# A new order of events and new buffer places for a fused delta-rule attention and FFN kernel, with 30 instead of 49 groups of products of zeros

## The chip, the cores and the metric

The kernel runs on one core of one Trainium2 chip. The metric is the device time of one execution in microseconds (us). Before the change three runs took 625.97, 626.17 and 628.18 us; the median is 626.17 us.

## The reference

The inputs are q, k, v of shape (4, 8, 768, 48), beta (4, 8, 768), and two weights, w_in (384, 2048) and w_out (2048, 384). They come as float64 words that the kernel takes apart itself.

```python
k_n = k / (norm(k, axis=-1) + 1e-6)
for t in range(S):                       # S = 768
    y[:, :, t] = q[:, :, t] @ state      # 48 x 48 state for each of 32 heads
    v_old = state^T k_n[:, :, t]
    state = state + beta_t * outer(k_n[:, :, t], v_t - v_old)
x = y, heads side by side, (3072, 384)
h = x @ w_in
sp = where(h > 20, h, log1p(exp(min(h, 20))))
out = (h * tanh(sp)) @ w_out
```

So: a delta-rule recurrence over 768 tokens, and a feed-forward layer (FFN) with a mish activation behind it.

## The kernel before

**Tiling.** The recurrence is cut into 12 chunks of 64 tokens, n = 0 to 11. The 32 heads lie in two halves of 16 (h = 0, 1 stand for eight head pairs each). For a chunk the steps are: `s_a` and `s_b` (products ta and tb, the two parts of a triangular inverse), `s_gq` (products gq of k with the state and q), `s_z` (products pz of the inverse with v), `s_y` (products py, the attention output), `s_s` (products ps, the state's update) and `s_pg` (products pg of k with k). The state of chunk n lies in the tiles xx0 and xx1, one for each half; the gq of chunk n+1 reads what ps of chunk n has put there.

**Solves.** `early(g)` (L1403) solves the triangular systems of the two chunks 2g and 2g+1 together on VectorE: it turns the k of both chunks (L1411), adds up their pg products into d (L1397), transposes d into gt (L1447), and runs a chain of multiplications and additions (pr at L1494, gt at L1496), closes with a multiplication (L1498) and transposes back (L1516 and following); copies on GpSimd (`place`, L1535) bring the result to where pz reads it. "Solve 1" is early(1), for chunks 2 and 3.

**FFN.** `moe(n)` (L1822) does a chunk's 256 rows in eight parts fp: `g1` makes the products h (18 of them, 128x256, L1842), ScalarE makes e = mish(h) (L1857) and a rounded copy g (L1858), VectorE the remainder (L1859); `g2` adds 12 products acc (128x384, L1876). h0_1 is part 1 of chunk 0, and g2.0_1 or "the first acc" is named in the same way. The attention output is split for it into x0 (L1756, ScalarE) and x1 (L1757, VectorE).

**Weights.** `convert` (L1285) makes two float32 parts of each float64 weight tile: ri is a piece of w_in, ro of w_out. A clip (L1292), for some a rounding (L1300), a shift (L1305) and a combination (L1309) run on VectorE, the rest on ScalarE, GpSimd and, through products with an identity, on TensorE (L1321, L1325). These conversions stand between the first chunk's attention steps.

**Evictions.** gq is taken out by VectorE (L1712, L1715), pz by ScalarE in two copies (L1737), ps by VectorE (L1783; for chunk 0 by ScalarE), q of chunk 1 is turned by VectorE (L1615).

**Order.** Each engine runs its instructions in the order in which the program issues them. That order is a table: `TT` (L37) gives each event (a load, a conversion, a step with its attention and FFN parts, an eviction) its places in the whole program, and `SLOT` gives each tile its buffer in its pool. `put` pushes the pieces of an event with their place on a heap, and `run` (L2096) takes them off in that order; a piece whose `needs` are not given yet waits until they are. `load` (L1231) issues nearly all loads on SyncE's queue. `keep_warm` (L1900) issues products of a tile of zeros, whose result nobody reads, at the places that TT gives to the groups in `TN['warm']`:

```python
for _ in range(n):
    nc.tensor.matmul(warm, zb[:, 0:P], zb[:, :512], start=True, stop=True)
```

Of the kernel before, what the change touches and what calls it, by code (L numbers as in the profile page):

```python
# [29 lines left out]
def bcast_in(ap, n):  # L30
# [106 lines left out]
    'ats_gq[0,1].0>2': [160],
    'cv7': [161, 194, 201, 238, 239, 277, 335, 346, 968],
    'cv27': [162, 186, 243, 314, 560, 563, 572, 573, 577],
    'loadp': [169],  # L140
    'ats_a[0,1]': [170],
    'ats_a[0,0]': [171],
    'ats_a[0,1].0>1': [172],
    'warm11.9': [173],
# [2003 lines left out]
```

## Time and profile before

| | |
|---|---|
| median of three runs | 626.17 us |
| the profiled execution | 628.7 us |
| its span | 627.0 us |
| mean granted TensorE clock | 0.977 |
| TensorE (PE) busy | 588.8 us, 94% |
| VectorE (DVE) busy | 401.5 us, 64% |
| ScalarE (ACT) busy | 271.7 us, 43% |
| GpSimd (POOL) busy | 89.1 us, 14% |

The profile is one execution, taken by the hardware profiler; its span runs from the first to the last instruction, and 1.7 us of the execution's time lie around it. PE is TensorE, DVE VectorE, ACT ScalarE, POOL GpSimd, SP (and SPq, its queue) SyncE. PEclk is the clock that the throttle granted, as a part of full speed. A busy TensorE need not be at its peak. A time on an engine that others don't wait for costs nothing. Lines such as L1411 are lines of the kernel before; the changed kernel's lines behind its tables are lower by 19.

### The profile page before, as it was taken

How to read it: one execution, taken by the hardware profiler on the slowest of the kernel's cores; microseconds unless marked ns; L12 is line 12 of the kernel's file. 1: busy time of each engine (PE TensorE's matmuls, PEld its weight loads, DVE VectorE, ACT ScalarE, POOL GpSimd, SP SyncE). 2: the span in 40 equal slices, each digit the busy share in tenths (PEclk: the TensorE clock that was granted, in tenths of full speed). 3: DMA queues.
4: the chain of work that ended last, by engine and by line, in shares of the span. 5: the costliest groups of instructions: out<-in, count | busy, mean ns of one | idle time of the engine just before them, and what ended most of it. 6: DMA issues, size and time to landing. Idle time of an engine off the chain costs nothing.

```text
span 627.0 us, 22002 instructions
## 1 busy us (share of the span) xinstructions
PE 588.8 (94%) x9622; PEld 546.0 (87%) x9634; DVE 401.5 (64%) x873; ACT 271.7 (43%) x515; POOL 89.1 (14%) x142
## 2 busy tenths in 40 slices
PE   7679788998999999999999999999999999999997
PEld 5346577998899889998988998899999999999997
DVE  2898578997589966898465996456985434331110
ACT  4358748554443354424434434344333432333331
POOL 5120123315020030012101012101002110000000
PEclk9699979998999989999999999999999999999999
DMA  9998854862431421321523402420204121110011
GB/s 252 252 278 192 149 99 72 123 101 52 62 53 28 74 45 23 63 49 15 86 40 55 85 1 40 71 49 3 51 2 78 27 48 33 26 28 1 1 25 26
DMA packets 161775, 43.21 MB, mean 69 GB/s; under 512 B 149008, under 2 KB 157664, under 8 KB 161680
## 3 DMA queue, kind: packets, MB, share of 16 engines
q1 hardware_dynamic: 156640, 36.93, 30.5%
q0 software_dynamic: 2784, 4.29, 4.2%
q8 instruction: 76, 1.25, 0.8%
q10 hardware_dynamic: 2256, 0.59, 0.4%
q14 instruction: 19, 0.16, 0.1%
HBM read 32.87 MB, written 4.72 MB: 60 GB/s over the span
## 4 chain that ended last, share of the span: by engine, by line
PE 62%; DVE 18%; DMA 6%; ACT 4%; SPq 4%; issue 4%; POOL 1%; DVEq 0%; ACTq 0%; POOLq 0%
PE acc L1876 24%; PE h L1842 20%; DVE pr L1494 4%; DVE gt L1496 4%; SPq L1233 4%; PE py L1626 3%; PE pz L1626 3%; PE gq L1626 3%; DVE g L1859 2%; PE ps L1791 2%; PE pg L1393 1%; DMA kt<-in_k_dram 1%; DVE d L1516 1%; DMA ri<-in_moe_w_in_dram 1%; POOL tt L1535 1%
## 5 line engine op out<-in xcount | busy, mean ns | idle before, releaser
L1876 PE MATMUL acc<-wo,g 128*128 128x384 f32 x1152 | 217.9, 342 | 1.0 <-issue 1.0
L1842 PE MATMUL h<-x,wi 128*128 128x256 f32 x1728 | 217.2, 282 | 1.5 <-ACT e L1857 1.5
L1842 PEld LDWEIGHTS h<-x,wi 128*128 128x128 f32 x1728 | 209.8, 189 | 4.3 <-ACT e L1857 2.0
L1876 PEld LDWEIGHTS acc<-wo,g 128*128 128x128 f32 x1152 | 200.6, 190 | 4.8 <-issue 2.3
L1859 DVE TENSOR_TENSOR g<-e,g 128x512 fp32r<-128x512 f32 x96 | 66.4, 696 | 77.9 <-ACT g L1858 77.6
L1857 ACT ACTIVATE e<-h 128x512 f32<-128x512 f32 x96 | 57.0, 598 | 130.6 <-PE h L1842 97.6
L1858 ACT CAST g<-e 128x512 fp32r<-128x512 f32 x96 | 59.0, 620 | 28.4 <-PE acc L1876 25.9
L1494 DVE TENSOR_TENSOR pr<-gt 128x58 f32<-128x58 f32 (+9 forms) x164 | 56.6, 345 | 4.3
L1496 DVE TENSOR_TENSOR gt<-gt,pr 128x58 f32<-128x58 f32 (+9 forms) x164 | 54.7, 333 | 4.7
L1626 PE MATMUL gq<-xx,kt 48*64 48x112 f32 (+1 forms) x768 | 52.0, 273 | 2.8 <-issue 1.6
L1626 PEld LDWEIGHTS pz<-vt,tt 64*64 64x64 f32 x768 | 44.0, 135 | 7.7 <-issue 2.3
L1626 PE MATMUL pz<-vt,tt 64*64 64x48 f32 x768 | 48.3, 226 | 1.7 <-ACT tt L1691 1.5
L1626 PEld LDWEIGHTS gq<-xx,kt 48*64 48x64 f32 x768 | 45.6, 135 | 4.5 <-issue 2.7
L1737 ACT COPY xx<-pz 64x384 f32<-64x384 f32 x48 | 22.7, 474 | 56.4 <-PE ta L1641 19.1
L1715 DVE TENSOR_TENSOR xx<-gq,amask 64x256 f32<-64x256 f32 x96 | 40.2, 418 | 0.7
L1604 POOL TENSOR_TENSOR vt<-vt,ne 128x384 f32<-128x384 f32 x24 | 21.5, 902 | 125.2 <-DMA vt<-in_v_dram 102.0
L1535 POOL COPY tt<-d 32x512 f32<-32x512 f32 x40 | 26.7, 667 | 79.2 <-DVE d L1516 45.3
L1712 DVE TENSOR_TENSOR vt<-vt,gq 128x192 f32<-128x192 f32 x44 | 15.5, 353 | 34.5 <-PE gq L1626 22.2
L1611 DVE STREAM_TRANSPOSE xx<-xx 128x1024 f32<-128x1024 f32 x20 | 24.8, 1239 | 15.7 <-DMA xx<-in_q_dram 13.6
L1393 PE MATMUL pg<-kt 48*64 48x64 f32 x768 | 27.3, 221 | 4.3 <-DVE tt L1568 3.4
L1757 DVE TENSOR_TENSOR x<-py,x 128x384 fp32r<-128x384 f32 x24 | 13.3, 553 | 24.6 <-ACT x L1756 24.4
L1626 PE MATMUL py<-xx 128*32 128x64 f32 (+1 forms) x1536 | 27.0, 221 | 1.4 <-issue 1.4
(141 smaller groups left out, 600.5 us busy)
## 6 DMA issues: line engine op xcount, KB each, us to landing
ro<-in_moe_w_out_dram SPq DMA_DIRECT2D x32, 192.0 KB, 4.6
ri<-in_moe_w_in_dram SPq DMA_DIRECT2D x24, 256.0 KB, 4.7
kt<-in_k_dram SPq DMA_DIRECT2D x76, 64.0 KB, 3.0
vt<-in_v_dram SPq DMA_DIRECT2D x48, 96.0 KB, 3.1
xx<-in_k_dram SPq DMA_DIRECT2D x48, 96.0 KB, 2.9
out_dram<-o SPq DMA_DIRECT2D x46, 96.0 KB, 2.2
xx<-in_q_dram SPq DMA_DIRECT2D x80, 32.0 KB, 2.3
wo<-mo POOLq DMA_DIRECT2D x9, 192.0 KB, 3.3
```

Source lines behind the costliest of these rows:

```text
L1233: m = (nc.scalar if turns[0] else nc.sync).dma_start(out=dst, in_=src)
L1393: nc.tensor.matmul(ps[64 * hh:64 * hh + C, p % 8, :], k, k, start=True, stop=True)
L1494: nc.vector.tensor_tensor(out=pv, in0=nj, in1=xj, op=ALU.mult)
L1496: nc.vector.tensor_tensor(out=below, in0=below, in1=pv, op=ALU.add)
L1535: nc.gpsimd.tensor_copy(out=tt2[r, t2, :, c0:c0 + 32], in_=dts[g][r, t2])
L1626: last[:] = [nc.tensor.matmul(*a, start=True, stop=True)]
L1715: nc.vector.tensor_tensor(out=x[r, p4, hh, D:D + C], in0=ps[r, :, d:], in1=bcast_mid(amask[r], 4), op=ALU.mult)
L1842: nc.tensor.matmul(h[:, f2, :], wt["i", f * P // WI * NCH + c][:, i2, f0:f0 + P], x[:, c, :], start=(i == 0), stop=(i == 3 * NCH - 1))
L1857: for d, f in ((0.7, lambda: nc.scalar.activation(e, h, AF.Mish)), (0.7, lambda: nc.scalar.copy(out=gg[:, 0], in_=e)), (0.8, lambda: nc.ve ...
L1858: (0.7, lambda: nc.scalar.copy(out=gg[:, 0], in_=e)),
L1859: (0.8, lambda: nc.vector.tensor_tensor(out=gg[:, 1], in0=e, in1=gg[:, 0], op=ALU.subtract))):
L1876: nc.tensor.matmul(acc[t], gg[:, a, f2, ts_], wt["o", f][:, i2, :], start=(f == 0 and i == 0), stop=(f == NF - 1 and i == 2))
```

## The change

No operation of the computation is changed. The table TT is written anew for all events (940 keys and 1552 places, where there were 959 and 1571), and SLOT has another buffer for 331 of its 551 tiles. TN['warm'] has 30 groups with 59 products of zeros, where there were 49 with 95.

```diff
-    'loads': [257],
+    'loads': [266],
...
-    'loadk2': [258],
+    'loadk2': [220],
...
-    'loadk3': [276],
+    'loadk3': [260],
...
-    'loado9': [254],
+    'loado9': [276],
...
-    'loadp': [169],
+    'loadp': [282],
...
-              warm=[(0.501,2),(0.502,2),(0.503,2),(0.6,2),(0.601,2),(0.602,1),(11.501,2),(11.502,2),(11.503,2),(11.6,2),(11.602,2),(11.603,2),(11.7,2),(11.701,2),(11.8,2),(11.803,2),(11.9,2),(11.901,2),(11.902,2),(11.903,2),(12.0,2),(12.003,2),(12.1,2),(12.101,2),(12.102,2),(12.2,2),(12.201,2),(12.3,2),(12.4,2),(12.401,2),(29.5,2),(29.501,2),(32.2,2),(36.4,2),(36.401,2),(40.201,1),(43.6,2),(46.6,2),(46.601,1),(50.02,2),(50.04,2),(50.05,2),(50.11,2),(50.12,2),(50.13,2),(50.14,2),(50.15,2),(50.16,2),(50.17,2)],
+              warm=[(0.501,2),(0.502,2),(0.503,2),(0.6,2),(0.601,2),(0.602,1),(11.5,2),(11.503,2),(11.6,2),(11.7,2),(11.701,2),(11.901,2),(11.902,2),(11.903,2),(12.0,2),(12.002,2),(12.003,2),(12.1,2),(12.3,2),(12.301,2),(12.4,2),(29.5,2),(30.6,2),(32.2,2),(36.4,2),(50.02,2),(50.07,2),(50.09,2),(50.11,2),(50.14,2)],
```

(loads is the load of q1, q of chunk 1; loadp that of vt1, v of chunk 1; loado9 a weight piece, ro9.)

What that moves is seen in each engine's order of instructions, of which three places follow.

SyncE's queue of loads, before (kt2 and kt3 are k of chunks 2 and 3, ro weight pieces; vt1 stands ten rows ahead of this):

```order
L1233 DMA ro9_1050<-in_moe_w_out_dram 128x384 x2
L1233 DMA q1_1055<-in_q_dram 32x16x32 x8
L1233 DMA kt2_1064<-in_k_dram 32x16x32 x8
L1233 DMA kt3_1113<-in_k_dram 32x16x32 x8
L1233 DMA ro14_1126<-in_moe_w_out_dram 128x384 x2
L1233 DMA xx1_107<-in_k_dram 64x8x48 x2
```

and now:

```order
L1214 DMA kt2_881<-in_k_dram 32x16x32 x8
L1214 DMA ro10_1051<-in_moe_w_out_dram 128x384 x2
L1214 DMA kt3_1055<-in_k_dram 32x16x32 x8
L1214 DMA q1_1071<-in_q_dram 32x16x32 x8
L1214 DMA ro9_1124<-in_moe_w_out_dram 128x384 x2
L1214 DMA ro14_1146<-in_moe_w_out_dram 128x384 x2
L1214 DMA vt1_0_1149<-in_v_dram 64x8x48 x2
L1214 DMA vt1_1_1152<-in_v_dram 64x8x48 x2
```

kt2 and kt3 stand ahead of q1, ro9 and vt1.

VectorE from the turn of kt2 and kt3 on, before (tt2 and tn are of chunk 1's inverse; mo, spare are combinations of weight pieces):

```order
L1411 STREAM_TRANSPOSE kt2_1064<-kt2_1064 128x1024
L1411 STREAM_TRANSPOSE kt3_1113<-kt3_1113 128x1024
L1568 TENSOR_TENSOR tt2_110<-tt2_110,mb1_1_1210 128x8x16
L1570 STREAM_TRANSPOSE tn0_455<-tt2_110 128x512
L1305 TENSOR_SCALAR ri6_987<-ri6_987 128x512
L1305 TENSOR_SCALAR ro15_611<-ro15_611 128x384
L1309 SCALAR_TENSOR_TENSOR mo4_1295<-ro4_776 128x384
L1712 TENSOR_TENSOR vt1_0_727<-vt1_0_727,gq1_00_1301 128x192
L1715 TENSOR_TENSOR xx0_106<-gq1_00_1301,amask_87 64x4x64 x2
```

and now:

```order
L1392 STREAM_TRANSPOSE kt2_881<-kt2_881 128x1024
L1392 STREAM_TRANSPOSE kt3_1055<-kt3_1055 128x1024
L1281 SCALAR_TENSOR_TENSOR ro12_745<-ro12_745 128x384
L1286 TENSOR_SCALAR ro6_470<-ro6_470 128x384
L1273 TENSOR_SCALAR ro10_1051<-ro10_1051 128x384
L1290 SCALAR_TENSOR_TENSOR spare_113<-ri6_161 128x512
L1286 TENSOR_SCALAR ro8_392<-ro8_392 128x384
L1738 TENSOR_TENSOR x1_0_1085<-py0_0_1086,x0_0_1084 128x3x128
L1596 STREAM_TRANSPOSE xx0_106<-q1_1071 64x8x64 x2
L1273 TENSOR_SCALAR ro9_1124<-ro9_1124 128x384
```

The turns come after 119 rows, where it was 131; behind kt3's turn stand conversions and x1_0, and 32 rows in all up to gt1, where there were 23.

TensorE at the end of chunk 5's first pz group, before (gq5 and ta6 run between its products, and py5_0 reads what ScalarE copies out of pz5_0):

```order
L1626 MATMUL gq5_11_4615<-xx1_107,kt5_2098 64x112
L1641 MATMUL ta6_4582<-d3_3191,at6_3192 33x32 x2
L1876 MATMUL acc0_3_4259<-wo14_2331,g3_7_4397 128x384 x3
L1876 MATMUL acc0_3_4259<-wo15_2328,g3_7_4397 128x384 x3
L1876 MATMUL acc1_3_4260<-wo14_2331,g3_7_4397 128x384 x3
L1876 MATMUL acc1_3_4260<-wo15_2328,g3_7_4397 128x384 x3
L1626 MATMUL py5_0_4680<-xx0_106 32x64 x12
```

and now:

```order
L1622 MATMUL ta6_4540<-d3_3108,at6_3109 33x32 x2
L1607 MATMUL pz5_0_4538<-vt5_0_3618,tt2_110 64x48
L1607 MATMUL gq5_11_4573<-xx1_107,kt5_2385 64x112
L1622 MATMUL ta6_4540<-d3_3108,at6_3109 33x32 x2
L1607 MATMUL py5_0_4624<-xx0_106 32x64 x12
L1607 MATMUL py5_0_4624<-xx0_106 16x64 x4
```

The acc group that stood between pz5_0 and py5_0 stands elsewhere. The same holds for py6_0, py7_0 and ps4_1; py1_1 and py11_0 have one py group between them and their pz.

## Rows read from the trace of the kernel before

**Rows 1.** The page: busy time by engine; TensorE's granted clock in 40 slices.

```profile
PE 588.8 (94%) x9622; PEld 546.0 (87%) x9634; DVE 401.5 (64%) x873; ACT 271.7 (43%) x515; POOL 89.1 (14%) x142
...
PEclk9699979998999989999999999999999999999999
```

**Rows 2.** Stages: length; busy PE, PEld, DVE, ACT, POOL; PEclk; DMA share; GB/s.

```profile
15.00:30.00 15.00, 8.43 (x81) 5.75 (x81) 12.45 (x40) 5.31 (x12) 3.12 (x4) 0.66 1.05 253
...
75.00:90.00 15.00, 9.44 (x215) 8.45 (x214) 10.51 (x22) 6.57 (x14) 3.18 (x5) 0.77 0.75 135
90.00:105.00 15.00, 13.32 (x166) 10.88 (x164) 11.50 (x31) 13.61 (x26) 5.69 (x7) 1.00 0.30 50
...
135.00:150.00 15.00, 13.41 (x219) 12.91 (x219) 13.74 (x28) 7.20 (x14) 7.66 (x11) 0.93 0.19 30
150.00:165.00 15.00, 13.15 (x307) 11.78 (x306) 6.17 (x13) 7.34 (x15) 1.05 (x3) 0.96 0.28 48
```

**Rows 3.** The same table, stages of 30 us, the four with gaps.

```profile
195.00:225.00 30.00, 27.72 (x464) 26.29 (x463) 28.23 (x62) 9.94 (x21) 5.76 (x10) 0.97 0.43 71
...
285.00:315.00 30.00, 28.25 (x639) 26.12 (x637) 17.25 (x29) 13.14 (x26) 6.23 (x11) 1.00 0.34 54
315.00:345.00 30.00, 27.49 (x633) 25.69 (x634) 18.43 (x34) 12.55 (x23) 2.10 (x2) 1.00 0.30 48
...
375.00:405.00 30.00, 28.17 (x634) 26.32 (x633) 17.96 (x30) 12.36 (x24) 6.82 (x10) 1.00 0.33 49
```

**Rows 4.** Timeline of SyncE's load issues: start, us, what, count.

```profile
36.48 3.12 SPq L1233 DMA_DIRECT2D vt<-in_v_dram  x4
...
51.63 0.91 SPq L1233 DMA_DIRECT2D ro<-in_moe_w_out_dram  x2
52.58 9.25 SPq L1233 DMA_DIRECT2D q<-in_q_dram  x8
...
61.94 11.04 SPq L1233 DMA_DIRECT2D kt<-in_k_dram  x16
```

**Rows 5.** Timeline of VectorE: start, us, what, [idle before <-releaser].

```profile
70.36 1.25 DVE L1411 STREAM_TRANSPOSE kt<-kt 128x1024 f32<-128x1024 f32 x1 [0.25 <-DMA kt<-in_k_dram]
77.26 1.25 DVE L1411 STREAM_TRANSPOSE kt<-kt 128x1024 f32<-128x1024 f32 x1 [5.66 <-DMA xx<-in_k_dram]
...
81.84 1.42 DVE L1615 STREAM_TRANSPOSE xx<-q 64x512 f32<-64x512 f32 x2
...
87.95 0.48 DVE L1397 SCALAR_TENSOR_TENSOR d<-pg,sel,d 128x256 f32<-128x256 f32 x1 [2.13 <-ACT d L1396]
...
93.96 1.97 DVE L1447 STREAM_TRANSPOSE gt<-d 128x1024 f32<-128x1024 f32 x1
```

**Rows 6.** Chain that ended last, 140 to 161 us: start, us, what.

```profile
140.35 1.15 DVE gt L1498
...
151.31 0.29 PE pz L1626 x2
```

**Rows 7.** Line of the products of zeros: ns min/median/max, first and last start.

```profile
L1903 PE MATMUL warm<-zero x83: 379/379/634, 1.5 to 105.6; 128*128 128x512 bf16 x83
```

**Rows 8.** Chain, 376 to 402 us.

```profile
380.04 2.30 PE h L1842 x18
382.33 1.03 PE py L1626 x64
...
385.64 2.10 PE h L1842 x18
```

**Rows 9.** TensorE's waits, 160 to 560 us: total, times, longest.

```profile
PE ta L1641 <- DVE d L1516: 1.9, 2, 1.0
...
PE h L1842 <- ACT e L1857: 1.5, 2, 1.2
```

**Rows 10.** Line of the copies of pz: ns min/median/max, first and last start.

```profile
L1737 ACT COPY xx<-pz x48: 460/474/478, 57.1 to 558.5; 64x384 f32<-64x384 f32 x48
```

**Rows 11.** Timeline of TensorE: the second h group.

```profile
83.91 3.53 PE L1842 MATMUL h<-x,wi 128*128 128x256 f32 x18
```

More of the change, by code (lines that the diff above doesn't have):

```diff
@@ new lines @@
+    'loado8': [71],
+    'loadi5': [72],
+    'loadi7': [73],
+    'warm11.6': [74],
+    'warm0.503': [75],
+    'loadv': [77],
+    'scale_v(0,0)': [78],
+    'loado3': [83],
+    'turn_q0(1,).0>2': [88],
+    'loado7': [89],
+    'warm0.6': [91],
+    'warm12.3': [92],
+    'loadi3': [94],
+    'turn_q0(1,).0>1': [95],
+    'ats_gq[0,1]': [96],
+    'loado6': [101],
+    'warm11.903': [103],
+    'merge1': [104, 125, 223, 234],
+    'merge0': [105, 154, 157, 159],
+    'cv23': [107, 123, 126, 299, 430, 439, 440, 441, 459],
@@ L513 @@
[L513 to L527 removed]
+    'ats_y[1,0]': [438],
+    'ats_y[1,0].0>1': [444],
@@ new lines @@
+    'scale_v(2,0)': [445],
+    'g1.0.4.0>1': [446],
+    'ats_y[1,1]': [448],
+    'g1.0.5': [449],
+    'g1.0.5.0>1': [450],
+    'g1.0.4.0>2': [455],
+    'g1.0.4.0>3': [456],
+    'g2.0.2': [457],
+    'g2.0.3': [458],
+    'g2.0.4': [460],
+    'ats_y[1,1].0>1': [462],
+    'g1.0.5.0>2': [475],
+    'g1.1.0': [478],
+    'g1.1.0.0>1': [479],
+    'g1.0.5.0>3': [487],
+    'g1.1.0.0>2': [489],
+    'g1.1.0.0>3': [490],
+    'ats_s[1,1]+s_pg[4,1]': [491],
+    'ats_s[1,0]+s_pg[4,0]': [494],
@@ new lines @@
+    'turn_q(2,0)': [497],
+    'ats_s[1,1]+s_pg[4,1].0>1': [502],
+    'g1.0.6': [503],
+    'ats_s[1,0]+s_pg[4,0].0>1': [510],
+    'g1.0.6.0>1': [516],
+    'g1.0.6.0>2': [517],
+    'g1.0.6.0>3': [518],
+    'g1.0.7': [519],
+    'g1.0.7.0>1': [521],
+    'g2.0.5': [525],
+    'g1.1.1': [529],
+    'g1.1.1.0>1': [534],
+    'g1.1.1.0>2': [535],
+    'ats_gq[2,0]': [536],
+    'g2.0.6': [540],
+    'ats_gq[2,0].0>2': [541],
+    'g1.1.2': [542],
+    'g1.1.3': [544],
+    'g1.0.7.0>2': [552],
@@ new lines @@
+    'g1.5.4': [1039],
+    'g2.4.7.0>2': [1040],
+    'g2.5.0': [1041],
+    'turn_q(7,1)': [1042],
+    'g1.5.3': [1043],
+    'g1.5.3.0>1': [1044],
+    'g1.5.3.0>2': [1048],
+    'g1.5.3.0>3': [1049],
+    'g1.5.4.0>1': [1050],
+    'g2.5.1': [1051],
+    'g1.5.7': [1052],
+    'g2.5.2': [1053],
+    'g1.5.4.0>2': [1059],
+    'g1.5.4.0>3': [1060],
+    'g1.5.6': [1066],
+    'g1.5.7.0>1': [1067],
+    'g2.5.3': [1072],
+    'g2.5.4': [1073],
+    'g1.6.0': [1076],
+    'g1.5.5.0>2': [1082],
@@ new lines @@
+    'g1.11.2.0>2': [1494],
+    'g1.11.2.0>3': [1495],
+    'g1.10.7': [1496],
+    'g1.10.7.0>1': [1497],
+    'g1.10.7.0>2': [1498],
+    'g1.10.7.0>3': [1499],
+    'g1.11.5': [1500],
+    'g1.10.3': [1501],
+    'g1.10.3.0>1': [1502],
+    'g1.10.3.0>2': [1503],
+    'g1.11.4': [1504],
+    'g1.10.6': [1505],
+    'g1.10.3.0>3': [1506],
+    'g2.10.3': [1507],
+    'g1.10.5.0>2': [1508],
+    'g1.10.5.0>3': [1509],
+    'g1.11.4.0>1': [1510],
+    'g2.10.4': [1511],
+    'g1.11.5.0>1': [1512],
@@ new lines @@
+    'g1.11.5.0>2': [1513],
+    'g1.11.5.0>3': [1514],
+    'g1.10.6.0>1': [1515],
+    'g1.10.6.0>2': [1516],
+    'g1.10.6.0>3': [1517],
+    'g1.11.1': [1518],
+    'g1.11.1.0>1': [1519],
+    'g1.11.1.0>2': [1520],
+    'g2.10.5': [1521],
+    'g2.10.6': [1522],
+    'g2.10.7': [1523],
+    'g2.10.7.0>1': [1524],
+    'g2.10.7.0>2': [1525],
+    'g2.11.0': [1526],
+    'g1.11.4.0>2': [1527],
+    'g1.11.4.0>3': [1528],
+    'g1.11.3': [1529],
+    'g1.11.3.0>1': [1530],
+    'g1.11.3.0>2': [1531],
```

1739 lines of the change are left out of this document (801 added, 938 removed), and 136 rows, old and new, of the table SLOT.

## The prediction

> **What bounds the kernel now.** I read the page first, then the table by stage, then the waits and the chain inside the stages that the table singles out. In [rows 1] TensorE is busy for 588.8 of 627.0 us, so in most of the span only fewer or shorter products, or the ends of its few gaps, can give time. The slices of its clock say where that isn't so: they are full but for dips in the first sixth. The table [rows 2] shows two kinds of gap. Up to 105 us the engine is starved: busy 8.43, 9.44 and 13.32 of 15 us in three of the stretches, with DMA shares of 1.05 and 0.75 in the first two of these. A second, smaller gap stands in 135 to 165 us, 1.59 + 1.85 = 3.44 us. [Rows 3] give four later stretches of 30 us with 2.28, 1.75, 2.51 and 1.83 us of gap, 8.4 us together.
>
> Behind the early gap stands one load. SyncE issues its loads one behind the other [rows 4]: vt1 for 3.12 us from 36.48, ro9 for 0.91 us, q1 for 9.25 us, then kt2 and kt3 for 11.04 us together. VectorE turns kt2 at 70.36, then sits idle for 5.66 us until kt3 has landed at 77.26 [rows 5] (the row names the xx load behind it; by its output it is the turn of kt3). Everything of the second solve (chunks 2 and 3, "solve 1") hangs on that turn: its gt1 is written from 93.96 on [rows 5], its last multiply ends at 141.50, a transpose and copies on GpSimd follow, and the pz2 products start at 151.31 [rows 6]. That is the gap of 135 to 165 us: TensorE has run out of chunk 0's FFN and waits for solve 1. The later gaps are of the same kind, or waits of an attention step for the step before it.
>
> **The change, part by part.** The operations are the same, apart from 36 fewer products of zeros (95 before, 59 after).
>
> *Loads.* kt2 and kt3 now go ahead of q1, ro9 and vt1. The issue times bound what that gives kt3: at least q1 alone by kt's own rate, 11.04 / 2 = 5.5 us; at most all that was passed, 9.25 + 0.91 + 3.12 = 13.3 us. I take 5.5 + 3.12 = 8.6 us, leaving out ro9's 0.91 and q1's excess over kt's rate, so kt3 lands near 68.6. q1 and vt1 land later than before; both are first needed after kt3's turn, so I cost that at nothing: their cover is VectorE's list between the turn and gt1. If that cover goes (q1 later than about 77), gq1 and with it the d1 rows behind it are late next.
>
> *VectorE up to solve 1.* With kt3 there, VectorE itself is what remains. The order has 12 fewer rows ahead of the turns than before (119 for 131), but weight clips wait for other loads, and the first merge (tt2 with mb0) has 10 more rows ahead of it. The turn falls between 68.6 (landing) and 74; I take 71, about where the engine stood ready before (71.6, [rows 5]). Between the turn and gt1 stand now 32 rows, where there were 23. By the durations in [rows 5] and of their like: 19 conversions of 0.35 to 0.69, in all 8.6 us; four d rows of 0.48, 1.9; two q turns of 1.42, 2.8; two vt and two xx evictions, 0.34 and 0.85, 2.4; two x of 0.55 and one g of 0.68, 1.8. Sum 17.5 us. So gt1 starts at 71 + 1.25 + 17.5 = 89.8 us, against 93.96: 4.2 us earlier. Before, 3.6 us of waits lay in the same stretch (2.13 of it in [rows 5]); if they all came back, 0.6 us would be left, and if the turn is at 68.6 without them, 6.5 us.
>
> *Solve 1 itself.* It has 33 rows of other work between its steps instead of 31: one g more (0.68), two shifts (0.35 each), one combine less (0.6), so +0.8 us. Its end moves by 4.2 − 0.8 = 3.4 us. TensorE has the same work ahead of pz2_0 as before (the same groups, in another order), so the gap of 3.44 us at 135 to 165 can close only as far as the early gap closes too. It can: the early gaps of 75 to 105 us are 5.56 + 1.68 us and hang on the same turn. I take **−3.4 us** here, bounds −7 and +1.
>
> *Products of zeros.* They fill gaps; a row takes 0.38 us [rows 7]. 36 × 0.38 = 13.7 us would be the most, if they stood on the path, but VectorE sets the end of these stretches, so I take nothing; below nothing is the clock rival.
>
> *Order of attention and FFN groups.* A group of 12 or 18 FFN products is longer when it stands behind attention products: 2.30 against 2.10 us for h [rows 8]. The new order has 49 such changes of kind for 53: 4 × 0.2 = **−0.8 us**.
>
> *Spacing in the later chunks.* A state update ps of chunk n is now mostly followed by one more FFN group (2.1 us) before the gq of chunk n+1 that needs it. That bears on the gaps of [rows 3], 8.4 us. Of these I leave 1.9 us of waits for a solve's transpose and 1.2 us of one for a mish [rows 9], and take the rest as relieved: −5.3 us; none at the other end. Against it, six places lose the cover between a pz and the step that needs its copy: py5_0, py6_0, py7_0 and ps4_1 now follow their pz group at once, py1_1 and py11_0 after one py group (1.03 us, [rows 8]). ScalarE copies pz in two pieces of 0.474 us [rows 10]. With one FFN group as cover there is no wait: py7_0 starts at 382.33, as the h group behind pz7_0 ends [rows 8]. So a bare place costs between 0.47 and 2.1 us; nearest is the row of the two copies, 0.95, and with a handoff some 1.1: 4 × 1.1 + 2 × 0.1 = +4.6 us. Solves 3 and 4 hold two more g and one more kt turn, +1.3 us each; as solve 1's earlier end carries on to them I count a quarter of the two, +0.7. Together −5.3 + 4.6 + 0.7 = **0.0 us**, bounds −4 and +10. This is the weakest term.
>
> **The sum.** 628.7 (the profiled execution; its span is 627.0, 1.7 us lie around it) − 3.4 − 0.8 + 0.0 = 624.5. The profiled one is 2.5 us over the median of the three runs, 626.17, so on the median's footing 626.17 − 4.2 = **622.0 us**. Half a per cent, about what a measurement of this kernel can tell from no change, is 3.1 us: faster is under 623.0, slower over 629.3.
>
> **The rivals.** (1) *The clock falls for want of zero products.* In 15 to 30 us the granted clock was 0.66 with TensorE busy 8.43 of 15 us, in 75 to 90 us 0.77 with 9.44, and 1.00 in the next stretch with 13.32 [rows 2]: means over its two levels, 1.2 and 2.4 GHz. In the second dip an h group took 3.53 us [rows 11], for 2.30 behind attention products later [rows 8]: 1.2 us for each such group. The new order has fewer zero products and puts ten of them ahead of h0_1, none in the place of the 14 that stood ahead of the first acc. If three groups ran at the low clock and the gap ahead of solve 1's end doesn't hide them, 622.0 + 3.6 = 625.6 us. For it: fewer fillers in the very stretch that dipped. Against it: kt3's earlier landing takes away the idle that went before the dip. The Trainium skill, page TensorE: Matmul & The Clock Gate, section What's actually happening, calls the throttled clock the default, released by activity; the dips agree, 0.66 and 0.77 beside the idlest stretches, and by that rule alone taking fillers out of a starved stretch costs time.
>
> (2) *The bare evictions decide* (the other side). At py5_0, py6_0, py7_0 and ps4_1 TensorE waits for ScalarE's copy, and if a copy queues behind a mish row, each wait comes to its upper bound, 2.1 us, and the two near ones to 1.1: 8.4 + 2.2 = 10.6 us in place of 4.6. With both solves' 1.3 us showing in full, 2.6 for 0.7, and half of the relief, 2.7 for 5.3, the time is 622.0 + 6.0 + 1.9 + 2.6 = 632.5 us. With the solves and the relief as in that case it is slower than before at 1.1 us a place already; with both as in the forecast, from 2.1 us on. For it: a waiting TensorE holds up the FFN groups queued behind it too. Against it: ScalarE is busy for only 9.9 to 13.1 of 30 us [rows 3].
>
> (3) *The loads give nothing*: VectorE reaches kt3's turn at 75 because the early conversions, put ahead of the first merge, wait for their weights. Then gt1 stays near 94, the first term is +0.8 for −3.4, and the time 626.2 us.
>
> **How the numbers follow.** Forecast 0.50, rival 1 0.13, rival 2 0.17, rival 3 0.20. The forecast's own range is 622.0 − 5 to 622.0 + 3. With the first term's lower bound (−3.6 more) and the spacing's (−4 more), which would hardly come together, the low end is 615; the high end, 630, takes in rivals 1 and 3 and the lower half of rival 2. Faster: most of the forecast, 0.43 of 0.50, and part of rivals 1 and 3, 0.09 together, so 0.52. Slower: rival 2's 0.15, and 0.05 of rival 3, so 0.20. Same: 0.28.
>
> **What the changed profile would show.** kt3's turn without the 5.66 us of idle ahead of it, at 69 to 73 us; gt1 at 89 to 91; pz2_0 at 147 to 149 and less than 2 us of gap in 135 to 165; py5_0, py6_0 and py7_0 each with about 1 us ahead of it, released by the copy of pz on ScalarE; a clock slice under 0.9 after 75 us would speak for rival 1. I am wrong if gt1 isn't before 93, or if the time comes or goes after 165 us.

## The result and the profile after

The changed kernel took 633.05 us, the median of four runs (632.12 to 634.17); the kernel before, run beside it, 626.07 (four runs, 625.3 to 628.18). The ratio is 1.0107, with a 95% interval of 1.0075 to 1.0139: slower by 0.75 to 1.4%, where 622.0 was forecast and the range ended at 630. The profiled executions are 633.8 us (span 631.6) and 628.7 (627.0), so the traces show 4.6 us of span of a difference that is 7.0 between the medians. All ratios leave out executions in the chip's slower state; medians are those of all runs.

The page after, busy time, TensorE's clock and the costliest line's idle time, for [rows 1]:

```profile
PE 587.2 (93%) x9588; PEld 549.7 (87%) x9598; DVE 402.5 (64%) x873; ACT 274.5 (43%) x516; POOL 88.8 (14%) x142
...
PEclk9896979998999998999997999999999999999999
...
L1823 PE MATMUL h<-x,wi 128*128 128x256 f32 x1728 | 218.2, 283 | 4.9 <-ACT e L1838 4.6
```

TensorE has the same products to make but for 36 of zeros, and is busy for 587.2 us where it was 588.8. Products of zeros make up 16.4 us of that, for 23.9 before (where not all of them are recorded, 49 of 59 and 83 of 95), so the others took some 6 us longer: the time went into idling and into products at the lower clock. The clock row has dips that the row before lacks, in the 16th slice (8, from 237 us) and the 22nd (7, from 332 us), and h waits 4.6 us for a mish on ScalarE. The stages after, as in [rows 2]:

```profile
75.00:90.00 15.00, 11.27 (x269) 10.18 (x268) 11.77 (x25) 11.11 (x22) 5.29 (x7) 0.89 0.65 110
90.00:105.00 15.00, 14.67 (x194) 12.40 (x192) 11.07 (x27) 13.38 (x25) 3.62 (x5) 0.88 0.52 90
...
135.00:150.00 15.00, 13.54 (x222) 12.67 (x221) 14.24 (x29) 5.47 (x11) 6.55 (x11) 0.94 0.47 73
150.00:165.00 15.00, 15.00 (x314) 14.26 (x313) 7.90 (x15) 8.45 (x18) 2.19 (x4) 0.94 0.24 42
```

and those of 30 us, as in [rows 3], with the one of 225 to 255 us that was full before:

```profile
195.00:225.00 30.00, 28.96 (x444) 26.84 (x444) 27.69 (x64) 10.34 (x20) 3.65 (x7) 1.00 0.36 60
225.00:255.00 30.00, 24.19 (x587) 22.73 (x580) 15.67 (x26) 11.79 (x21) 4.56 (x6) 0.94 0.27 43
285.00:315.00 30.00, 29.10 (x649) 27.72 (x648) 20.28 (x34) 11.54 (x23) 6.14 (x10) 1.00 0.32 53
315.00:345.00 30.00, 25.72 (x545) 24.54 (x546) 13.43 (x23) 10.09 (x19) 1.70 (x3) 0.89 0.21 36
375.00:405.00 30.00, 28.69 (x536) 27.19 (x535) 22.37 (x44) 11.59 (x22) 4.76 (x8) 1.00 0.26 42
```

```profile
225.00:255.00 30.00, 30.00 (x651) 28.40 (x650) 17.98 (x34) 16.27 (x30) 1.67 (x2) 0.98 0.10 16
```

(the last row is the kernel before). Three of the four gaps of [rows 3] shrank: 2.28 to 1.04 us, 1.75 to 0.90, 1.83 to 1.31. But 225 to 255 us now holds a gap of 5.81 us, and 315 to 345 one of 4.28 for 2.51, both with a lower clock. TensorE's waits there, 225 to 350 us (total, times, longest):

```profile
PE h L1823 <- ACT e L1838: 4.3, 1, 4.3
PE gq L1607 <- issue: 3.8, 1, 3.8
PE py L1607 <- ACT xx L1718: 1.0, 2, 0.5
```

**Where the time went.** To place it I sum, at some points of the program, the shortest durations of all product groups done so far (h 2.10, acc 2.08, py 1.03 us and so on), and take this from the time at which the last of them ended: what is left is the time lost until then. The points are equal amounts of work in each kernel (a_both and a_best are two versions from the experiments below; each column is one profile):

| time lost (us) until | before | after | a_both | a_best |
|---|---|---|---|---|
| solve 1's result (90 us of work) | 59.1 | 60.5 | 58.7 | 60.6 |
| ahead of the gap in chunk 4 (165) | 70.7 | 68.2 | 66.2 | 68.7 |
| behind it (175) | 71.8 | 76.0 | 73.0 | 72.2 |
| ahead of the gap in chunk 6 (245) | 79.2 | 80.7 | 77.7 | 77.1 |
| behind it (260) | 82.0 | 88.1 | 79.5 | 78.9 |
| end (528) | 94.7 | 99.4 | 89.8 | 90.0 |

After against before: +1.4 up to solve 1, then −3.9, then +6.7 in chunk 4 (7.8 for 1.1), −2.7, +4.6 in chunk 6 (7.4 for 2.8), −1.4: together +4.7. Outside these two places, of 10 and 15 us of work, the new order is 6.6 us better in these two profiles.

**The gap of chunk 6** shows best how it comes about. Timelines after, of ScalarE (first row), VectorE and TensorE (last row): start, us, what, and in brackets the idle time before and what ended it.

```profile
333.55 0.48 ACT L1737 CAST x<-py 128x384 fp32r<-128x384 f32 x1 [8.20 <-PE h L1823]
...
334.06 0.56 DVE L1738 TENSOR_TENSOR x<-py,x 128x384 fp32r<-128x384 f32 x1 [7.98 <-ACT x L1737]
334.63 1.12 DVE L1764 TENSOR_TENSOR xx<-xx,ps 48x384 f32<-48x384 f32 x2
335.78 0.48 DVE L1378 SCALAR_TENSOR_TENSOR d<-pg,sel,d 128x256 f32<-128x256 f32 x1
336.18 1.24 DVE L1592 STREAM_TRANSPOSE xx<-xx 128x1024 f32<-128x1024 f32 x1
...
337.52 0.42 PE L1607 MATMUL gq<-xx,kt 48*64 48x112 f32 x1 [3.77 <-issue]
```

The x of an attention output has two buffers, taken in turn by chunks. The x of py6_0 goes where chunk 4's x lay, which all of chunk 4's h groups read. In the kernel before, the order is py6_0, h4_7: the last reader comes at once. Now h4_7 stands behind py6_0, g2.4_4, g2.4_5, ps6_0 and h5_1 and starts some 8 us after py6_0's end, and ScalarE's copy of py6_0 waits 8.20 us for it. Nobody wants that x yet. But behind the copy VectorE holds its own half of x, the state xx from ps6_0, a d, and the turn of chunk 7's q. All four stand still (7.98 us of idle), and the products gq7_00, which need state and q, come 3.77 us late; by the row they wait for "issue", and only the row ahead of them on VectorE tells why. Then the clock: it was 0.50 from 336 to 342 us, and the h group behind took 3.02 us for 2.10 to 2.30.

```profile
336.00:342.00 6.00, 4.48 (x129) 4.45 (x130) 3.22 (x6) 2.16 (x5) 0.00 (x0) 0.50 0.02 4
...
341.39 3.02 PE L1823 MATMUL h<-x,wi 128*128 128x256 f32 x18
```

**In chunk 4** the same wait stands at the head of a longer chain: x of py4_0 waits for h2_5, put behind it. On ScalarE's queue the mish e3_2, which frees a PSUM buffer for h3_0, stands behind that copy, and also behind the two rows that take out pg7_0 (d, and at, which waits for VectorE) and a cast. How much of the gap is the copy's, a_h25 tells below.

```profile
236.04 0.48 ACT L1737 CAST x<-py 128x384 fp32r<-128x384 f32 x1 [4.51 <-PE h L1823]
...
240.33 3.92 PE L1823 MATMUL h<-x,wi 128*128 128x256 f32 x18 [4.32 <-ACT e L1838]
...
237.00:240.00 3.00, 0.00 (x0) 0.00 (x0) 1.89 (x5) 1.20 (x3) 0.00 (x0) 1.00 0.44 66
240.00:243.00 3.00, 2.67 (x13) 2.67 (x14) 2.71 (x6) 1.49 (x3) 0.00 (x0) 0.57 0.88 140
```

h3_0 waits 4.32 us, and runs at 3.92 us for 2.10 to 2.30: in 237 to 240 us TensorE did nothing, and in 240 to 243 its granted clock was 0.57. The two levels are 1.2 and 2.4 GHz, 0.5 and 1 in these rows; so an idle of 4 us cost 1.6 us more in the group behind it here, and 0.7 in the h group of chunk 6.

### The profile page after: what moved, and what is told of

Its sections match the earlier page's. It is cut to its first block, busy times and chain, and to the rows that moved or that the text cites. A ratio compares the mean times of both kernels' runs of the same rounds, so it can differ in the third digit from the quotient of the medians.

```text
span 631.6 us, 21936 instructions
## 1 busy us (share of the span) xinstructions
PE 587.2 (93%) x9588; PEld 549.7 (87%) x9598; DVE 402.5 (64%) x873; ACT 274.5 (43%) x516; POOL 88.8 (14%) x142
## 3 DMA queue, kind: packets, MB, share of 16 engines
q8 instruction: 75, 1.23, 0.9%
## 4 chain that ended last, share of the span: by engine, by line
PE 68%; DVE 15%; SPq 5%; DMA 4%; issue 3%; ACT 2%; POOL 1%; DVEq 0%; ACTq 0%; POOLq 0%
PE acc L1857 25%; PE h L1823 25%; SPq L1214 5%; DVE gt L1477 4%; DVE pr L1475 4%; PE py L1607 3%; PE pz L1607 3%; PE gq L1607 3%; PE pg L1374 2%; DVE g L1840 2%; PE ps L1772 1%; PE warm L1884 1%; DMA ro<-in_moe_w_out_dram 1%; DMA kn<-in_k_dram 1%; DMA ri<-in_moe_w_in_dram 1%
## 5 line engine op out<-in xcount | busy, mean ns | idle before, releaser
L1477 DVE TENSOR_TENSOR gt<-gt,pr 128x58 f32<-128x58 f32 (+9 forms) x164 | 56.3, 343 | 4.4
L1693 DVE TENSOR_TENSOR vt<-vt,gq 128x192 f32<-128x192 f32 x44 | 15.5, 353 | 35.6 <-PE gq L1607 31.1
L1585 POOL TENSOR_TENSOR vt<-vt,ne 128x384 f32<-128x384 f32 x24 | 23.4, 980 | 100.7 <-DMA vt<-in_v_dram 61.9
L1374 PE MATMUL pg<-kt 48*64 48x64 f32 x768 | 31.6, 243 | 0.4 <-ACT xx L1718 0.2
L1374 PEld LDWEIGHTS pg<-kt 48*64 48x64 f32 x768 | 28.9, 156 | 1.3 <-DVE x L1738 0.3
```

The source lines that it names most:

```text
L1374: nc.tensor.matmul(ps[64 * hh:64 * hh + C, p % 8, :], k, k, start=True, stop=True)
L1477: nc.vector.tensor_tensor(out=below, in0=below, in1=pv, op=ALU.add)
```

## The experiments

Each edits places of the table only; "time" is the median, the ratio is to the kernel before, run on the same chip, with its 95% interval. The theory to begin with: the two gaps make the change slower, each by one late FFN group.

**a_h25**: h2_5 ahead of py4_0.

```diff
-    'g1.2.5': [770],
+    'g1.2.5': [764.5],
```

> The changed kernel (633.05 us) with one event moved: the h group h2_5, the last of chunk 2, goes ahead of py4_0 instead of behind ps4_0. Theory X (x buffers): the split of py4_0 writes the buffer that chunk 2's h groups still read, so ScalarE's copy x<-py4_0 waits for h2_5, and with it all that is queued behind it on ScalarE and VectorE; moved, that copy starts within 1 us of py4_0's end instead of 3.4 us after it, the 4.3 us gap ahead of h3_0 goes, and the time is 627 to 629 us. Rival S (spacing of the state): TensorE was out of ready work there whatever the copy does; the gap moves to the next gq or solve and the time stays within 1.5 us of 633.

631.16 us, 1.006 (1.0039 to 1.0081): a miss, and its interval overlaps the change's. The copy of py4_0 now starts within 0.1 us of py4_0's end, as wanted, and yet h3_0 still waits 3.27 us:

```profile
232.26 0.48 ACT L1737 CAST x<-py 128x384 fp32r<-128x384 f32 x1 [3.28 <-PE py L1607]
...
236.54 3.91 PE L1823 MATMUL h<-x,wi 128*128 128x256 f32 x18 [3.27 <-ACT e L1838]
```

So the late reader accounts for about 1 us of the 4.32; the rest is the chain of d, at, cast and e3_2 on ScalarE.

**a_h47**: h4_7 back behind py6_0.

```diff
-    'g1.4.7': [987],
+    'g1.4.7': [973.5],
```

> The changed kernel with one event moved: h4_7, the last h group of chunk 4, goes from behind h5_1 to between the two acc groups behind py6_0. Theory X: ScalarE's copy of py6_0 no longer waits 8.2 us for h4_7, the update of the state and the turn of q behind it come about 6 us earlier, the 3.8 us gap inside the pz6_1 group goes, and the clock dip at 333 to 341 us with it; time 627.5 to 629.5 us. Rival S: the gq of chunk 7 still waits for its q load or for ps6_0, time 631.5 to 633.5 us.

626.95 us, 1.0005 (0.9976 to 1.0034). The 3.8 us wait of gq is gone from the list of waits, and with it one per cent of the time (1.0107 before this edit), 6 us for one place of one group, a little more than expected.

**a_both**: both.

> The changed kernel with both moves. Theory X: both gaps go, 633.05 minus 4.5 to 6 for each: 622 to 624.5 us, faster than the kernel before (626.1). Rival S: 630 us or more. Third possibility (solve-bound): the first gap's time is given back by solve 3, whose end is set by VectorE, and only one of the two gains stays: 627 to 629 us.

625.62 us, 0.9979 (0.9954 to 1.0004), above the 622 to 624.5 expected if both gaps closed: the one in chunk 4 stays. Of TensorE's waits from 160 us on it is the only one longer than 1.5 us:

```profile
PE h L1823 <- ACT e L1838: 3.6, 2, 3.3
PE py L1607 <- ACT xx L1718: 1.5, 3, 0.5
```

**b_h47late**: the same fault put into the kernel before.

```diff
-    'g1.4.7': [991],
+    'g1.4.7': [999.5],
```

> The kernel before (626.1 us) with the fault put in: h4_7 goes from right behind py6_0 to behind the two acc groups that follow ps6_0; ScalarE's and VectorE's orders are the same. Theory X: the copy of py6_0 waits for h4_7's end, state update and q turn follow, and the pz6_1 group gets a gap of 2.5 to 4 us; time 628.5 to 630.5 us. Rival S: nothing waits that didn't, 625.5 to 627 us.

631.99 us, 1.0086 (1.0058 to 1.0114), somewhat more than expected: the cause in chunk 6 from the other side. VectorE's x waits there too, and the time lost at this place is 8.7 us (245 to 260 us of work) for 2.8:

```profile
327.79 0.56 DVE L1757 TENSOR_TENSOR x<-py,x 128x384 fp32r<-128x384 f32 x1 [7.73 <-ACT x L1756]
```

**a_e32**: a_h47, and the mish e3_2 ahead on ScalarE's queue.

```diff
-    'g1.3.2.0>1': [774],
+    'g1.3.2.0>1': [765.5],
```

> The changed kernel with h4_7 moved as before (626.95 us in that run) and one more event: e3_2, the mish of h3_2, goes ahead of ScalarE's copy x<-py4_0; h2_5 stays behind ps4_0. h3_0 needs the PSUM buffer of h3_2, and e3_2 stood behind the copy of py4_0, the d and at of pg7_0 and a cast. Theory M (queue of the mish): the gap ahead of h3_0 goes though the copy still waits for h2_5; time 622 to 624 us. Rival X (copy alone): the gap stays at 3 us or more and the time within 1.5 us of 627.

626.24 us, 0.9992 (0.9965 to 1.002): a miss. h3_0's wait is gone and stands at the next group, the acc group g2.2_5 (3.73 us), whose g is queued behind the same copy.

**a_all**: a_both, with e3_2 at 764.7.

> All three moves: h2_5, h4_7 and e3_2. Theory M and X together: no gap over 1 us ahead of h3_0, time 621 to 623.5 us, the same as the run with e3_2 and h4_7 alone or up to 1 us less. Rival (solve-bound): solve 3 on VectorE takes the gain back by a longer wait for pz5_0, 625 us or more.

623.89 us, 0.9944 (0.9911 to 0.9976), just above what was expected. The gap has not closed; it is smaller, and at g2.2_5 as well:

```profile
238.98 3.94 PE L1857 MATMUL acc<-wo,g 128*128 128x384 f32 x12 [2.48 <-ACT g L1839]
```

**a_bare**: a_all, with an FFN group put as cover behind the pz of three bare places.

```diff
-    'g1.4.3': [922],
+    'g1.4.3': [916.5],
-    'g1.6.6': [1132],
+    'g1.6.6': [1126.5],
-    'g1.3.4': [791],
+    'g1.3.4': [789.5],
```

> The three moves, and an h group put back between pz5_0 and py5_0 (h4_3), pz7_0 and py7_0 (h6_6) and pz4_1 and ps4_1 (h3_4). Theory B (a bare place costs the copy's latency): the waits ahead of py5_0 and py7_0 (0.77 us each in the changed kernel) and of ps4_1 (1.2 us) go, against 0.2 us for each further change of kind: 1.5 to 2.5 us less than with the three moves alone. Rival: the state updates behind come 2.1 us later and the next gq waits for them, so that nothing or a loss of up to 2 us is seen.

628.78 us, 1.0036 (1.0008 to 1.0063), slower than a_all. The waits at py for the copy of pz fell from 1.5 us in all to 0.5, but acc waits 2.6 us for VectorE's remainder instead of 0.8, and pg 1.4 us for a copy (225 to 560 us):

```profile
PE acc L1857 <- DVE g L1840: 2.6, 3, 1.9
PE acc L1857 <- ACT g L1839: 2.5, 1, 2.5
PE pg L1374 <- ACT ax L1642: 1.4, 1, 1.4
```

So theory B missed, and the loss is larger than its rival had it. Here the bare places were cheaper than the groups that covered them; the three were not tried one by one.

**b_loads**: in the kernel before, kt2 and kt3 ahead of ro9 and q1 in SyncE's queue, and q1's first turn on VectorE behind kt3's.

```diff
-    'loadk2': [258],
+    'loadk2': [253.3],
-    'turn_q(1,0)': [275],
-    'loadk3': [276],
+    'turn_q(1,0)': [306.6],
+    'loadk3': [253.6],
```

> The kernel before with the loads alone changed: kt2 and kt3 ahead of ro9 and q1, and q1's first turn on VectorE behind kt3's. Theory L (kt3's load binds solve 1, as the prediction had it): the 5.7 us of idle ahead of kt3's turn goes, gt1 starts 3 to 5 us earlier, solve 1 ends 3 us earlier, time 622.5 to 624 us. Rival D (VectorE's and ScalarE's chain binds): the idle moves to the turn of q1 and to the waits for d, gt1 comes 0 to 2 us earlier, and the time is 625 to 627 us.

630.94 us, 1.006 (1.003 to 1.0091): a miss for both theories. The weight ro9 is late now, and VectorE's clip of it stops everything behind it; gt1 comes at 99.07.

```profile
70.98 0.36 DVE L1292 TENSOR_SCALAR ro<-ro 128x384 f32<-128x384 f32 x1 [7.93 <-DMA ro<-in_moe_w_out_dram]
```

**b_loads2**: the same with ro9 left ahead (loadk2 254.3, loadk3 254.6).

> The kernel before with kt2 and kt3 ahead of q1 alone (ro9 stays where it was) and q1's first turn on VectorE behind kt3's. In the run with ro9 passed too, VectorE sat idle for 7.9 us at ro9's clip and kt3's turn came later than before. Theory L: without that stall kt3's turn has no idle over 1 us ahead of it, gt1 starts 2 to 4 us earlier than 93.96 and the time is 623 to 625 us. Rival D: q1's turn or the copies for n=0 stall instead, gt1 within 1.5 us of 93.96 or later, 626 us or more.

627.49 us, 1.0009 (0.9987 to 1.0032). kt3 is turned at 73.26 us after 3.61 us of idle instead of 5.66, and q1 is late: the gq that need it wait 3.33 and 2.29 us. Solve 1's gt starts at 93.60, for 93.96 before, as rival D had it.

```profile
75.52 0.48 PE L1626 MATMUL gq<-xx,kt 48*64 48x112 f32 x2 [3.33 <-DVE xx L1615]
78.29 3.03 PE L1626 MATMUL gq<-xx,kt 48*64 48x112 f32 x29 [2.29 <-DVE xx L1615]
```

**a_g26**: a_all, with g2_6's cast and remainder earlier and g2_5's chain in its order.

```diff
-    'g1.2.6.0>2': [772],
-    'g1.2.6.0>3': [773],
+    'g1.2.6.0>2': [764.72],
+    'g1.2.6.0>3': [764.74],
-    'g1.2.5.0>1': [777],
-    'g1.2.5.0>2': [778],
-    'g1.2.5.0>3': [779],
+    'g1.2.5.0>1': [766.5],
+    'g1.2.5.0>2': [766.6],
+    'g1.2.5.0>3': [768.5],
```

> The three moves (h2_5, h4_7, e3_2; 623.9 us) and chunk 2's last mish chain freed: the cast and remainder of g2_6 and the mish, cast and remainder of h2_5 go ahead of chunk 4's d and at (pg7_0) on ScalarE and VectorE. Theory M2: with e3_2 moved, the gap had gone on to g2.2_5 (4.35 us), because g2_6's cast stood behind the copy of py4_0 and d, and e2_5 needs its buffer; freed, that gap falls under 1.5 us, of which the next wait (q of chunk 5, landed at 240.8 us) takes 2 us back: 621 to 622.5 us. Rival: what is gained is all given back at the pz4_1 group or by solve 3, 623.5 us or more.

626.9 us, 0.9988 (0.9959 to 1.0016): a miss. The gap left g2.2_5 and stood at gq5_00, 4.25 us lost. q of chunk 5 can only be loaded once py4_0 has read the state's buffer, and is turned on VectorE after that:

```profile
241.31 1.25 DVE L1592 STREAM_TRANSPOSE xx<-xx 128x1024 f32<-128x1024 f32 x1 [1.54 <-DMA xx<-in_q_dram]
```

Busy in 225 to 255 us stays at 26.64 us, with 26.80 in a_all. The gap has moved through three instructions, h3_0, g2.2_5 and gq5_00, without closing.

**a_best**: a_g26 with TensorE's order in chunk 4 as pz4_0, h2_5, py4_0, g2.2_4, ps4_0, h3_0, g2.2_5. Up to ps4_0 that is the order of the kernel before; behind ps4_0 the kernel before has g2.2_5 and g2.2_6, and h3_0 only after the next pz group.

```diff
-    'g2.2.4': [763],
+    'g2.2.4': [766.8],
-    'g1.2.5': [764.5],
+    'g1.2.5': [762.5],
```

> Edit: the events of a_g26, and in chunk 4 h2_5 goes behind pz4_0 and ahead of py4_0's remainders' reader: the order on TensorE is pz4_0, h2_5, py4_0, g2.2_4, ps4_0, h3_0, g2.2_5, that of the kernel before. Chain theory: TensorE loses time where the distance from a product to the one that needs its result is shorter than the chain of ScalarE, VectorE and DMA between them, whatever instruction stands there. From py4_0, behind which load_q(5,0) may be issued, to gq5_00 there are then about 2.1 us of products less in a_g26 and this order gives them back: the wait at pz4_1 and gq5_00 falls from 4.25 us in a_g26 to about 2 us, none of over 1 us appears at g2.2_5 or h3_0, and the time is about 2 us under a_all's 623.9, 621 to 623.5 (0.990 to 0.994 of the kernel before). Rival: the wait goes on to yet another instruction (h3_0, ps4_0 or gq5_00 still at 4 us), and the time stays at that of a_all and a_g26, 623.5 to 627.

621.96 us over nine runs, 0.991 (0.988 to 0.9939), as expected, though its interval overlaps a_all's. The stage has 27.36 us busy, at full clock; the wait at gq5_00 costs 1.68 us in the measure of the table above:

```profile
225.00:255.00 30.00, 27.36 (x631) 25.83 (x631) 19.41 (x36) 15.16 (x27) 5.18 (x7) 1.00 0.28 44
```

**a_warm**: a_all, with four products of zeros, a new group (60.0,4), ahead of chunk 1's tb.

```diff
-    'ats_b[1]': [336],
+    'ats_b[1]': [336], 'warm60.0': [335.5],
```

> The three moves (623.9 us) and four more products of zeros between gq1_01 and tb1, where TensorE waits 2.0 us and then runs pg3_0 and pg3_1 at the low clock (1.92 and 1.71 us for 0.93). Theory C (the clock costs there): pg3_0 and pg3_1 take under 1.1 us each, gt1 starts 1 to 2 us earlier, solve 1's end and the time fall by 1 to 1.5 us: 622.4 to 623 us. Rival: the fillers run at the low clock themselves and delay tb1, gt1 moves by less than 0.5 us, 623.5 to 625 us.

621.65 us over five runs, 0.9909 (0.9875 to 0.9943). The median is lower than a_all's, within overlapping intervals, and not by the mechanism expected: solve 1's pg products still run at the low clock, as in a_all (3.69 us) and after (3.68), for 2.10 before:

```profile
83.14 3.68 PE L1374 MATMUL pg<-kt 48*64 48x64 f32 x64
```

**The start.** gt of the first solve begins at 17.7 to 19.9 us in ten profiles of the new order and at 15.0 to 15.5 in four of the old. Candidates were undone in the changed kernel: 12 fewer products of zeros ahead of the first real one (**f_warm** puts them back, as a group (60.1,12)), ScalarE's second table load of 1.28 us and beta's load ahead of k's (**f_act**), and both (**f_all**); **b_cold** takes 12 such products, six groups of warm, from the kernel before.

```diff
-    'warm0.501': [0],
+    'warm0.501': [0], 'warm60.1': [0.5],
...
-    'loada': [18],
+    'loada': [4.5],
-    'loadb': [1],
+    'loadb': [19.5],
```

> Edit: the changed kernel with 12 more products of zeros ahead of the first real product, 14 in all as in the kernel before (the change has 2). Front theory: the first solve's gt begins at 17.7 to 19.9 us in all ten kernels of the new order that were profiled and at 15.0 to 15.5 in the four of the old. Part of it is the clock: with 2 products of zeros the two kp groups take 1.93 us each, with 14 they take 1.04 and 1.06; and pg took 7.00 us in the changed kernel's profile, 3.95 before. With 14 the kp groups take 1.0 to 1.1, pg 3.95, gt begins at 16.4 to 17, gt of solve 1 1.5 to 2.5 us earlier than the 92.85 of the changed kernel, and the time is 630.5 to 631.5 against 633.05. Loads rival: the first 45 us are bound by the loads (DMA share 0.90 to 1.01 per stage); gt of the first solve comes earlier, kt3 and gt of solve 1 don't, and the time stays at 633.

> Edit: the changed kernel with ScalarE's table preload ahead of its first copy, and the load of beta behind the copies of the first chunks' k, both as in the kernel before. Front theory: the changed order loads ScalarE's tables twice (1.28 us each), the second time between the last two copies of kt and the first d, and issues beta's load (0.87 us) ahead of k's on ScalarE's queue. Without both gt of the first solve begins 1.3 to 2.1 us earlier (16 to 17.5 us, later where pg runs at the low clock), and the time falls by as much, to 631 to 632. Loads rival: as in f_warm, time 633.

> Edit: both edits, of f_warm and of f_act. Front theory: gt of the first solve begins at 15.0 to 15.6 us as in the kernel before, 3.2 us earlier than the mean of the ten kernels of the new order (18.4); VectorE's list, which sets the start of solve 1 now that kt3 is in time, moves up by that, and the time is 633.05 - 3.2 = 629.8 us, 629 to 630.7; the two gaps in chunks 4 and 6 stay. Loads rival: gt of the first solve moves, solve 1 doesn't, 632 to 634.

> Edit: the kernel before with 2 products of zeros ahead of its first real product instead of 14. Front theory: the kp groups take 1.9 us each instead of 1.05, and gt of the first solve begins 1.7 us later or more (16.8 to 19); but the kernel before waits 5.66 us for kt3 at its turn, so that this is hidden, and the time stays within 0.2% of before (625.5 to 627.5). Rival: everything that starts late ends late, 628 to 630 (1.003 to 1.006).

631.98 us (1.0062, 1.0035 to 1.0088), 634.21 (1.0086, 1.0055 to 1.0117), 633.01 (1.0074, 1.0047 to 1.0102) and 627.07 (0.9975, 0.9944 to 1.0006). In f_all gt of the first solve starts at 15.37 us, 4.5 earlier than in the change's profile, and solve 1's at 91.63, only 1.2 earlier: on the way VectorE waits for loads that did not come sooner.

```profile
41.84 0.36 DVE L1273 TENSOR_SCALAR ro<-ro 128x384 f32<-128x384 f32 x1 [3.56 <-DMA ro<-in_moe_w_out_dram]
...
68.00 1.25 DVE L1392 STREAM_TRANSPOSE kt<-kt 128x1024 f32<-128x1024 f32 x1 [1.12 <-DMA kt<-in_k_dram]
```

So the times of f_act and f_all go with the loads rival: the start is late, and nearly free. f_warm lies between the two theories, and its profile has solve 1's gt at 88.09; but a_bare, with no edit at the start, has it at 88.61, so such a difference between two profiles shows nothing. b_cold agrees with a start that is nearly free. Its first kp products take twice as long (16 in 3.92 us, for 8 in 1.04 before), and its time is that of before: the wait for kt3, still 5.42 us, hides it.

```profile
5.95 3.92 PE L1366 MATMUL kp<-ident,kn 128*112 128x128 f32 x16 [3.38 <-DMA kn<-in_k_dram]
...
78.31 1.25 DVE L1411 STREAM_TRANSPOSE kt<-kt 128x1024 f32<-128x1024 f32 x1 [5.42 <-DMA xx<-in_k_dram]
```

**f_top**: a_best with the zeros of f_warm and of a_warm (edits as shown there).

> Edit: the order of a_best, with 12 more products of zeros at the start (as in f_warm) and 4 ahead of chunk 1's tb (as in a_warm). Clock theory: f_warm and a_warm, each with a median below that of the kernel without the added zeros (631.98 for 633.05, 621.65 for 623.89, both within their intervals), gain by a higher clock ahead of the 78th microsecond; together on a_best that is 1 to 3 us, a time of 619 to 621 and a ratio to the kernel before of 0.985 to 0.989. Rival: these differences are the spread of the start from run to run, since VectorE and the loads set the end of the front; the ratio stays at a_best's 0.991 within its interval (0.988 to 0.994).

620.65 us over six runs, 0.9903 (0.9875 to 0.9932), which its interval does not tell from a_best's 0.991. It bears on what a_warm left open: in this profile solve 1's pg products do run nearly as fast as in the kernel before, 2.30 us for a_best's 3.68, and the ratio stays.

```profile
86.12 2.30 PE L1374 MATMUL pg<-kt 48*64 48x64 f32 x64
```

Both versions beat both kernels.

## Why the prediction was wrong

**The step that failed is the spacing in the later chunks**, "Together −5.3 + 4.6 + 0.7 = 0.0 us". It asked of each attention product how far behind its producer it now stands on TensorE. It did not ask what else a moved FFN group releases, nor what the group itself waits for. The two places cost +4.6 us (chunk 6) and +6.7 (chunk 4) in the profiles, 11.3 together, and no rival named them. In chunk 6 the cause is shown: h4_7 is the last reader of a buffer that a copy on ScalarE must write, and that copy's wait of 8.20 us is handed to all that is queued behind it. Moving this one group back (a_h47) takes 6 us off, moving it away in the kernel before (b_h47late) adds 5. In chunk 4 it is shown in part. The same wait for h2_5 is about 1 us of the 4.32 (a_h25). For the rest, the new order puts h3_0 and g2.2_5 close behind ps4_0, while the mish and the casts that they need stand on ScalarE behind rows that wait for VectorE; the wait moved from one to the other as each was freed, and the moves of a_best together brought the place from 7.8 to 3.5 us, for 1.1 before. With both places mended in this way the new order does come to 0.991 (a_best), near the 622.0 us of the forecast, which is 0.993 of 626.17, but by other terms than those of its sum.

**The rest of that step** came out better than forecast. Behind solve 1 and outside the two places the change gains 3.9 + 2.7 + 1.4 = 8.0 us, where −0.8 (changes of kind) and 0.0 were forecast; without these 8 us, which the forecast did not have either, the miss would have been larger. How much of this is spacing and how much the fewer changes of kind was not taken apart. The bare places themselves were sized well: py5_0, py6_0 and py7_0 lost 0.77 us each and ps4_1 1.23, for 1.1, and the waits at py for the copy of pz are 0.5 us each. Rival 2, in which these decide, came nearest in time (632.5 us), but by luck: its waits for the copy did not come to 2.1 us, and covering three of the places made the kernel slower (a_bare).

**The loads, forecast at −3.4.** The first link held: kt2 and kt3 are turned one behind the other without the 5.66 us of idle [rows 5], kt3 at some 70.7 us for the 71 of the forecast. SyncE has issued kt3's load by 61.6 us, for 73.0 before, so at the turn VectorE's own list binds.

```profile
56.28 5.36 SPq L1214 DMA_DIRECT2D kt<-in_k_dram  x8
...
69.53 2.36 DVE L1392 STREAM_TRANSPOSE kt<-kt 128x1024 f32<-128x1024 f32 x2
...
84.54 0.35 DVE L1693 TENSOR_TENSOR vt<-vt,gq 128x192 f32<-128x192 f32 x1 [1.68 <-POOL vt L1585]
...
90.48 0.48 DVE L1378 SCALAR_TENSOR_TENSOR d<-pg,sel,d 128x256 f32<-128x256 f32 x1 [1.31 <-ACT d L1377]
...
92.85 1.95 DVE L1428 STREAM_TRANSPOSE gt<-d 128x1024 f32<-128x1024 f32 x1
...
141.48 1.22 DVE L1479 TENSOR_TENSOR gt<-gt,y 128x1024 f32<-128x1024 f32 x1
```

gt1 starts at 92.85 for 89.8 forecast (88.0 to 93.5 in the nine a_ profiles of this order, and 91.79 in b_h47late, whose start is that of the kernel before, so one pair of profiles says little here). In its way stand waits that the sum had left out: 1.68 us for v of chunk 1, loaded later and scaled on GpSimd, and 0.55 + 1.31 + 0.76 us for d rows, whose pg products ran at the low clock. "I cost that at nothing" was wrong for vt1 here and for q1 in b_loads2. From gt1's start to its last multiply's end the solve takes 142.70 − 92.85 = 49.9 us for 141.49 − 93.96 = 47.5: +2.3 for the +0.8 forecast, 0.9 of it GpSimd's answer (a wait of 2.29 for 1.38 us). This term is the steady one: the solve takes 49.8 to 51.0 us in all fourteen profiles of the new order and 47.5 to 48.1 in all five of the old. So solve 1 ends 1.2 us later than before in this pair of profiles, and pz2_0 starts at 152.38 us for 151.31. This is near rival 3's value for the term (+0.8), by other means: kt3's turn came at 70.7 us, not at 75. With the loads alone moved in the kernel before (b_loads2) nothing is gained either: 1.0009.

**The gap of 135 to 165 us** did close, from 3.44 to 1.46 us, but not through an earlier pz2_0: 150 to 165 us is full now, with the work behind solve 1 in another order.

**Products of zeros, forecast at 0.** Right within what the runs can tell: 12 or 4 more of them changed the time by no more than the intervals (f_warm, a_warm, f_top), and 12 fewer in the kernel before likewise (b_cold). Rival 1's signs were there, pg at 3.68 us for 2.10 and kp at 1.93 for 1.04. The slow pg does make VectorE wait for d on the way to gt1, yet with pg at 2.30 us (f_top) the ratio did not move by more than its interval. (The prediction read the clock of the kernel before as full behind the first sixth; its row [rows 1] has an 8 in the 10th and in the 15th slice too.) The Trainium skill, page TensorE: Matmul & The Clock Gate, section What's actually happening, calls the throttled clock the default, released by activity: kp in b_cold agrees, and so does the clock of 0.50 that 336 to 342 us show behind the gap of chunk 6. At the start, where loads and VectorE set the end, the slow products cost no time that the runs can tell.

**What stays open.** Why chunk 4 still loses 3.5 us in a_best, for 1.1 before: q of chunk 5 comes late in a_g26 and a_best (an earlier load would need another buffer for the state, which was not tried), and the order of the kernel before behind ps4_0, g2.2_5 and g2.2_6 with h3_0 later, was not tried either. Open too is the 2.3 us by which the medians of the first comparison differ by more than its profiles.

## What to carry to other kernels

When a group is moved, ask not only who waits for its result but which buffer it is the last to read, who writes that buffer next, and what is queued behind the writer on its engine: here that third question was worth about 6 us for one group in chunk 6, the first about 1 us a place. A wait named "issue" or a mish is often the end of such a chain; follow the queue back to the instruction with the long idle. After removing one link look at the whole stage's busy time, not at the instruction: in chunk 4 the wait moved on through three instructions without closing.

## What was not expected of the hardware

A late start cost little where loads follow it: gt of the first solve 4.5 us earlier (f_all) came with 1.2 us at the next solve and no gain in time. Idle time of TensorE was paid for twice: after a wait of 4.32 us an h group took 3.92 us for 2.10 to 2.30, and the clock read 0.57 there. And executions of the same kernel differ by some us: the kernel before had medians of 625.84 to 628.36 us in seven comparisons, which is why versions are compared here by their ratios.
